# Attention with decay and a spectral mix on one core: the loads of v move from SyncE's DMA queue to GpSimd's

## The chip, the cores and the metric

The kernel runs on one core of a Trainium2 chip. The metric is the device time of one execution in microseconds. Each engine works through its own instructions in program order; a DMA is issued by an engine (here SyncE, called SP in the profile, or GpSimd, called POOL), and 16 DMA engines then move the data.

## The reference, cut to what matters

Two computations follow each other. The first is causal attention with a forgetting decay, for 8 batches and 8 heads, 576 positions, head size 64:

```python
scores = scale * np.matmul(q, k.transpose(0, 1, 3, 2))
cum = np.cumsum(np.log(np.clip(f, 0.0001, 1.0)), axis=-1)
decay = cum[:, :, :, None] - cum[:, :, None, :]
attn = softmax(where(causal, -1e9, scores + decay))
x = matmul(attn, v)          # then (batch, position, 8*64)
```

The second takes x (8 x 576 x 512), transforms it along the positions, multiplies its first 64 modes by complex matrices `w_r`, `w_i` (each 64 x 512 x 512 in float32, 64 MiB), transforms back to y, and gives `u + max(u @ w_ch, 0)` with u = x + y.

## The kernel before, in words

The order of all work is the program's order on each engine (`tc.manual_schedule()`, line 59): nothing is reordered.

**Attention, lines 442 to 493.** Two heads of one batch make a pair; there are 32 pairs, and iteration i of the main loop works on several of them at once: it loads pair i+3 (`load_qk`, `load_v`, lines 450 and 451), issues a tile of w where the plan says so (`issue_w`, line 453), scales v of pair i+1 (`scale_v`, line 455), computes the scores of pair i (`scores`, `mask`), the product with v of pair i-1 (`av`, `norm`), the transposes of q and k of pair i+1 (`trans`), the transform of pair i-2 (`dft`), and from iteration 10 on one early part of the product with w (`spec_early`, line 492).

- `load_qk` (line 99) makes two loads on GpSimd's queue, q and k of two heads, which are turned from float32 into bf16 on the way: 64 partitions, two rows of 2304 bytes read for each. Four buffers.
- `load_v` (line 110) makes four loads, two for each head: a large one of 128 x 4 rows (128 KB) and a small one of 64 rows (16 KB). A row is 64 float32 numbers, 256 bytes. They go into one of four buffers `vbuf[i % 4]`, tile name `vst` in the profile. Before the change they are issued on SyncE's queue.
- `issue_w` (line 128) makes two loads on GpSimd's queue, one of `w_r` and one of `w_i` (1 MiB read, 512 KB written as bf16 each; 128 x 4 rows). There are six buffers (`NW = 6`) for 64 such tiles. The plan (lines 439 to 441) issues one tile in each of the iterations 0 to 5, none in 6 to 10, and one in each of 11 to 32. The tile of iteration 11 takes the buffer that `spec_early` frees in iteration 10.
- `scale_v` (line 309) multiplies v by the decay weights `wT` on GpSimd, into one of three buffers `vs`, and so frees the buffer of v. It waits for v to have landed, and for `av` of three pairs before.

So GpSimd's instructions in iteration i are, in this order: q, k of pair i+3; a tile of w; scale_v of pair i+1. SyncE has only f (line 157), v, and the output at the end.

**Before the loop, lines 155 to 179.** GpSimd issues the loads of q and k of pairs 0 to 2, and between them makes the constants: the identity matrix `ident_bf`, the positions `s_i` (an iota, line 161, from which VectorE and ScalarE derive the transform's basis), `ident_f`, `trimask` and others, and then the load of `w_ch` (line 179). The calls of `load_v` for pairs 0 to 2 stand between these lines (158, 163, 167).

**Mode product, lines 497 to 607.** The remaining 42 tiles of w are loaded and multiplied with the transformed x, beside products with `w_ch`. **Output, lines 637 to 671**: the last modes are added and the result is written on SyncE's queue.

Of the kernel before, what the change touches and what calls it, by code (L numbers as in the profile page):

```python
# [23 lines left out]
def kernel(  # L24
# [11 lines left out]
    nc = tc.nc  # L36
# [73 lines left out]
    def load_v(i):  # L110
        g, b = pairs[i]
        vt = vbuf[i % VB]
        for hp in range(2):
            nc.sync.dma_start(
                vt[:, 4 * hp : 4 * hp + 4, :],
                v[b, 2 * g + hp, 0:512, :].rearrange("(c p) d -> p c d", p=128),
            )
            nc.sync.dma_start(
                vt[64 * hp : 64 * hp + 64, 8, :], v[b, 2 * g + hp, 512:576, :]
            )  # L120

# [34 lines left out]
    ft = ssb.tile([BH, S], F32, name="ft")  # L156
    nc.sync.dma_start(ft[:], f.rearrange("b h s -> (b h) s"))
    load_v(0)
    masks.make_identity(nc, ident_bf[:])
    s_i = ssb.tile([128, NSB], I32, name="s_i")  # L160
    nc.gpsimd.iota(s_i[:], pattern=[[128, NSB]], base=0, channel_multiplier=1)
    load_qk(1)
    load_v(1)
    masks.make_identity(nc, ident_f[:])
    masks.make_upper_triangular(nc, trimask[:], val=1.0, diag=True)
    load_qk(2)
    load_v(2)
    nc.gpsimd.memset(tri4[:], 0.0)
    nc.gpsimd.tensor_copy(tri4[0:64, 0, :], trimask[0:64, 0:64])
# [532 lines left out]
```

## Time and profile before

| what | value |
|---|---|
| median of 2 runs | 483.69 us (483.61 to 483.76) |
| the profiled execution: its own time | 485.75 us |
| its span, first to last instruction | 484.0 us |
| mean granted TensorE clock | 0.81 of full speed |
| busy: PE, DVE, ACT, POOL | 355.0, 263.7, 193.8, 184.1 us |
| read from HBM, written | 163.73 MB, 9.44 MB |
| v loads, large: number, KB, median time to landing | 64, 128 KB, 10.6 us |
| v loads, small | 64, 16 KB, 10.6 us |
| q and k loads | 64, 144 KB, 14.5 and 14.7 us |
| w loads | 128, 512 KB, 19.8 and 20.0 us |

How to read it: PE is TensorE, DVE VectorE, ACT ScalarE, POOL GpSimd, SP SyncE. A DMA that an engine issues appears twice: as a short instruction on the engine's timeline (its issue), and as a landing later. The DMA lines of the profile give the busy share of the 16 DMA engines in 40 slices, in tenths, and for each queue the packets, the MB written and the share of time that its packets took; the shares may add up to more than 100%, since packets of one engine overlap. The chain of waits follows the work that ended last back to what released it; a piece such as "DMA w" in it is the time from issue to landing.

### The profile page before, as it was taken

To read this page: it belongs to the slowest core of one execution; us is meant where nothing else is said; L and a number is where in the kernel's file an instruction comes from. 1 tells how busy PE (TensorE), PEld (TensorE's weight loads), DVE (VectorE), ACT (ScalarE), POOL (GpSimd) and SP (SyncE) were. 2 spreads that over 40 slices of the span, in tenths; PEclk is the share of its full clock that TensorE was granted. 3 is DMA by queue.
4 is the path that set the end of the run, shared out by engine and by line. 5 is a ranking of instruction groups with operands and counts; after the bars stand their busy time and mean duration, and the time that the engine had idled before them with its cause. 6 is when DMAs were issued, how large, how long until landed. Compare 5 with 4: busy or idle time off the path is not lost.

```text
span 484.0 us, 8618 instructions
## 1 busy us (share of the span) xinstructions
PE 355.0 (73%) x3387; PEld 175.1 (36%) x3396; DVE 263.7 (54%) x618; ACT 193.8 (40%) x300; POOL 184.1 (38%) x274
## 2 busy tenths in 40 slices
PE   1268779997686876768968577668756687986994
PEld 1135555564353533434524133223322232432331
DVE  4979988996465555747843112122120255453785
ACT  5246555674445444523502201222102255552773
POOL 8827544763544545355433322332233233200000
PEclk9999895998757667876967957787767599797998
DMA  8999999899999999999999999999999999993687
GB/s 161 203 197 198 197 198 181 137 196 197 196 196 197 197 198 197 199 197 203 206 206 207 206 206 207 206 206 206 207 206 206 206 206 208 206 206 52 238 300 245
DMA packets 121288, 96.65 MB, mean 200 GB/s; under 512 B 42336, under 2 KB 116576, under 8 KB 121248
## 3 DMA queue, kind: packets, MB, share of 16 engines
q0 software_dynamic: 77328, 77.08, 95.3%
q1 hardware_dynamic: 43920, 19.03, 19.2%
q8 instruction: 26, 0.43, 0.3%
q14 instruction: 14, 0.11, 0.1%
HBM read 163.73 MB, written 9.44 MB: 358 GB/s over the span
## 4 chain that ended last, share of the span: by engine, by line
DMA 68%; PE 14%; issue 6%; DVE 5%; POOL 3%; ACT 3%; DVEq 0%; POOLq 0%
DMA w<-in_moe_w_i_dram 41%; DMA qk<-in_k_dram 13%; DMA w<-in_moe_w_r_dram 12%; PE pav L388 2%; PE tp L299 2%; DMA out_dram<-o_sb 2%; ACT et L350 2%; PE sps L343 2%; PE U L648 1%; PE pd L415 1%; PE Z L648 1%; PE A L146 1%; POOL w L135 1%; POOL vs L312 1%; PE U L654 1%
## 5 line engine op out<-in xcount | busy, mean ns | idle before, releaser
L350 ACT ACTIVATE et<-sps 128x1024 bf16<-128x1024 f32 x96 | 94.3, 1025 | 69.2 <-PE sps L343 66.3
L135 POOL DMA_DIRECT2D w<-in_moe_w_r_dram x64 | 48.4, 756 | 118.5 <-DMA w<-in_moe_w_r_dram 41.9
L135 POOL DMA_DIRECT2D w<-in_moe_w_i_dram x64 | 47.8, 746 | 95.9 <-DMA w<-in_moe_w_i_dram 82.7
L146 PE MATMUL A<-w,XS 128*32 128x512 bf16 x512 | 50.6, 463 | 38.4 <-DMA w<-in_moe_w_i_dram 25.4
L304 DVE COPY qkT<-tp 128x640 bf16<-128x640 bf16 x64 | 49.2, 769 | 37.7 <-PE tp L299 37.6
L541 ACT CAST XW<-pxw 128x512 bf16<-128x512 f32 (+1 forms) x40 | 23.4, 585 | 106.8 <-PE pxw L534 106.8
L299 PE MATMUL tp<-ident_bf,qk 128*64 128x128 bf16 x576 | 35.6, 264 | 37.2 <-DMA qk<-in_k_dram 33.8
L388 PE MATMUL pav<-vs,et 128*128 128x65 bf16 (+1 forms) x896 | 61.2, 214 | 0.9 <-DVE et L359 0.8
L388 PEld LDWEIGHTS <-et 128*128 128x128 bf16 (+1 forms) x896 | 44.2, 115 | 29.4 <-issue 25.9
L594 DVE TENSOR_TENSOR Yb<-A,yacc 128x512 bf16<-128x512 f32 x16 | 11.1, 692 | 71.6 <-PE A L146 71.6
L534 PE MATMUL pxw<-wch,xT 128*128 128x512 bf16 (+1 forms) x152 | 45.5, 451 | 1.7 <-DVE xT L525 1.3
L343 PE MATMUL sps<-qkT 64*128 64x512 bf16 (+4 forms) x320 | 44.4, 344 | 1.7 <-DVE qkT L304 1.5
L312 POOL TENSOR_TENSOR vs<-vst,wT 128x576 bf16<-128x576 f32 x32 | 37.6, 1175 | 18.0 <-PE pav L388 12.8
L299 PEld LDWEIGHTS <-qk 128*64 128x64 bf16 x576 | 23.9, 132 | 42.9 <-issue 33.0
L578 DVE TENSOR_TENSOR XW<-pz,XW 128x512 bf16<-128x512 f32 (+1 forms) x40 | 27.0, 690 | 21.3 <-PE pz L577 21.1
L403 DVE TENSOR_TENSOR x_all<-pav,rcp 128x384 bf16<-128x384 f32 (+2 forms) x96 | 36.2, 377 | 3.4
L525 DVE COPY xT<-ptr 128x576 bf16<-128x576 bf16 x32 | 14.7, 458 | 39.7 <-PE ptr L520 39.5
L422 DVE CAST XS<-pd 128x192 bf16<-128x192 f32 x32 | 32.6, 1032 | 0.0
L146 PEld LDWEIGHTS <-XS 128*32 128x32 bf16 x512 | 10.7, 98 | 59.2 <-issue 54.0
L665 DVE SCALAR_TENSOR_TENSOR o_sb<-Z,u_sb 128x512 f32<-128x512 f32 (+1 forms) x40 | 25.6, 685 | 10.7 <-ACT u_sb L664 6.8
L415 PE MATMUL pd<-bas,x_all 128*128 128x192 bf16 (+1 forms) x160 | 28.6, 302 | 0.9 <-DVE x_all L403 0.5
L534 PEld LDWEIGHTS <-xT 128*128 128x128 bf16 (+1 forms) x160 | 17.3, 117 | 26.6 <-issue 15.2
(113 smaller groups left out, 479.6 us busy)
## 6 DMA issues: line engine op xcount, KB each, us to landing
w<-in_moe_w_r_dram POOLq DMA_DIRECT2D x64, 512.0 KB, 19.8
w<-in_moe_w_i_dram POOLq DMA_DIRECT2D x64, 512.0 KB, 20.0
vst<-in_v_dram SPq DMA_DIRECT2D x64, 128.0 KB, 10.6
out_dram<-o_sb SPq DMA_DIRECT2D x16, 512.0 KB, 2.9
qk<-in_q_dram POOLq DMA_DIRECT2D x32, 144.0 KB, 14.5
qk<-in_k_dram POOLq DMA_DIRECT2D x32, 144.0 KB, 14.7
vst<-in_v_dram SPq DMA_DIRECT2D x64, 16.0 KB, 10.6
out_dram<-o_sb SPq DMA_DIRECT2D x4, 256.0 KB, 3.2
```

Of the source, the lines that this page charges most:

```text
L135: nc.gpsimd.dma_start(w8[:, t, :, :], src[4 * u : 4 * u + 4, dc * 128 : (dc + 1) * 128, :].rearrange("m p e -> p m e"),)
L146: nc.tensor.matmul(A[32 * j : 32 * j + 32, :], lhsT=XS[:, dc, c0 : c0 + 32], rhs=w8[:, t, j, :], start=(first and t == 0), stop=(last and ...
L299: nc.tensor.transpose(tp[64 * hp : 64 * hp + 64, r - r0, :, :].rearrange("p n c -> p (n c)"), qk[:, hp, r * 64 : r * 64 + 64], ident_bf[:, :],
L304: nc.vector.tensor_copy(st[i]["T"][:].rearrange("p n (c r) -> p n c r", r=9)[:, :, :, r0:r1], tp[:, 0 : r1 - r0, :, :].rearrange("p r n c ...
L312: nc.gpsimd.tensor_tensor(vs[:, :, 0:Dh], vbuf[i % VB][:], _strided(wT[:, i, :], [[1, 9], [0, Dh]]), ALU.mult)
L343: nc.tensor.matmul(ps[:, hp, c : c + n], lhsT=KT[sl, jb * 128 : jb * 128 + 128], rhs=QT[sl, i0 : i0 + n], start=True, stop=True,)
L350: nc.scalar.activation(st[i]["et"][:, T, :, :], ps[:], ACT.Exp, scale=scale)
L388: nc.tensor.matmul(pav[:Ms, sb % 3, hp, :], lhsT=eblk(i, hp, jb, sb), rhs=rhs, start=(jb == 0), stop=(jb == sb),)
L403: nc.vector.tensor_tensor(x_all[:ns, b, lo:hi, g * 128 : g * 128 + 128].rearrange("p s (h d) -> p s h d", h=2), pav[:ns, lo % 3 : lo % 3 + ...
L415: nc.tensor.matmul(pd[:], lhsT=x_all[:ns, b, sc, g * 128 : g * 128 + 128], rhs=bas3[:ns, sc, :, :], start=(sc == 0), stop=(sc == NSB - 1),)
L422: nc.vector.tensor_copy(XS[:, g, 0 : 24 * NM].rearrange("p (m c b) -> p c m b", c=3, b=8)[:, :, :, b], pd[:])
L534: nc.tensor.matmul(pxw[:Ms, :], lhsT=xT[:, eb, sb * 128 : sb * 128 + Ms], rhs=wch[:, eb, :], start=(eb == 0), stop=(eb == NEB - 1),)
```

## The change

The four loads of `load_v` are issued by GpSimd instead of SyncE. Rows, sizes, buffers, and the place of the calls in the program stay the same.

```diff
@@ -111,11 +111,11 @@
         g, b = pairs[i]
         vt = vbuf[i % VB]
         for hp in range(2):
-            nc.sync.dma_start(
+            nc.gpsimd.dma_start(
                 vt[:, 4 * hp : 4 * hp + 4, :],
                 v[b, 2 * g + hp, 0:512, :].rearrange("(c p) d -> p c d", p=128),
             )
-            nc.sync.dma_start(
+            nc.gpsimd.dma_start(
                 vt[64 * hp : 64 * hp + 64, 8, :], v[b, 2 * g + hp, 512:576, :]
             )
```

GpSimd's instructions in iteration i are then: q, k of pair i+3; the four loads of v of pair i+3; a tile of w; scale_v of pair i+1. Before the loop, the four loads of each of the pairs 0 to 2 stand between the constants.

## The prediction

> **What bounds the kernel now.** I read the page first: is one resource full nearly all the time?
>
> ```profile
> DMA  8999999899999999999999999999999999993687
> ...
> q0 software_dynamic: 77328, 77.08, 95.3%
> q1 hardware_dynamic: 43920, 19.03, 19.2%
> ...
> DMA 68%; PE 14%; issue 6%; DVE 5%; POOL 3%; ACT 3%; DVEq 0%; POOLq 0%
> ```
>
> The DMA engines are full from 2 us to about 437 us, except near 80 to 88 us. q0 is GpSimd's queue (q, k, w), q1 is SyncE's (v, the output). POOL, which will issue the v loads, is only 38% busy; that average is taken apart below. The chain of waits, in order of time, shows how the queue is throttled:
>
> ```profile
> 118.91 16.56 DMA w<-in_moe_w_r_dram
> 135.51 0.49 issue
> 136.00 16.45 DMA w<-in_moe_w_r_dram
> 152.50 0.49 issue
> 152.98 0.77 POOL w L135
> ...
> 246.81 20.05 DMA w<-in_moe_w_i_dram
> 267.15 20.06 DMA w<-in_moe_w_i_dram
> 287.49 20.06 DMA w<-in_moe_w_i_dram
> ```
>
> A w_r load is issued 0.5 us after the w_r load of two iterations before has landed. With q, k, w_r, w_i per iteration that is the load eight places back. Later, with w alone, eight loads are in flight again: 20.34 us between pieces, 2.54 us per load. So POOL has at most eight loads out. The period in the attention stage is (152.98-118.91)/4 = 8.5 us; with w alone it is 20.34/4 = 5.1 us per tile of two loads. The timeline of POOL shows one iteration:
>
> ```profile
> 139.13 0.75 POOL L135 DMA_DIRECT2D w<-in_moe_w_i_dram  x1 [2.36 <-DMA w<-in_moe_w_i_dram]
> 139.89 1.16 POOL L312 TENSOR_TENSOR vs<-vst,wT 128x576 bf16<-128x576 f32 x1
> 141.00 0.23 POOL L315 CAST vs<-wT 128x9 bf16<-128x9 f32 x1
> 141.13 0.65 POOL L105 DMA_DIRECT2D qk<-in_q_dram  x1
> 141.78 0.61 POOL L105 DMA_DIRECT2D qk<-in_k_dram  x1
> 144.47 0.77 POOL L135 DMA_DIRECT2D w<-in_moe_w_r_dram  x1 [2.08 <-PE pav L388]
> ```
>
> POOL works 4.1 us of 8.5 and waits the rest for landings. (The releaser PE pav is only the event that came last; the chain shows the landing.) Last, the DMA view of two windows, 75.7 to 76.1 us (nearly only v moves) and 142.5 to 144.5 us (v beside w):
>
> ```profile
> q1 hardware_dynamic: 263, 0.06, 73.9%
> q0 software_dynamic: 12, 0.01, 25.9%
> ```
> ```profile
> q0 software_dynamic: 315, 0.31, 92.1%
> q1 hardware_dynamic: 315, 0.08, 29.7%
> ```
>
> Beside w the queues alternate one packet to one (315 and 315). A v packet of 256 B then takes 0.297x16x2000/315 = 30 ns; nearly alone it takes 0.739x16x400/263 = 18 ns.
>
> **The change, part by part.** Removed: 128 issues on SP (0.4 to 0.6 us each), which nothing but v waits for; worth nothing in themselves. SP keeps f and the output, whose first issue comes after 445 us. Also lost is SP's freedom: today v(i+3) goes out as soon as scale_v(i-1) has freed its buffer, an iteration ahead of POOL's order. This costs nothing by itself: on POOL v(i+3) is still issued two iterations before scale_v(i+3), 16 us against a landing time of some 8.
>
> Moved onto q0, transfers. Of the 8.5 us period w takes 5.1; q and k read 0.56 MiB against w's 2 MiB, 1.43 us at the same rate; 2.0 is left for v. A set of v (four loads) has 1152 rows, 72 per engine: 28 ns per row. In one queue the alternation is gone, and I take 18 to 20 ns, the row nearest in size: 72x19 ns = 1.37, with 0.08 for completions 1.45 us. Saving s = 0.55 us per set. Bounds: 28 ns as now, s = 0; or w's byte rate (2048 B read in 79 ns), 10 ns, s = 1.2. That a row costs more on this queue is not excluded: the nearest q0 row, of q and k, costs 88 ns, but it reads 2304 B at w's own byte rate, so I give that end little chance. From the first w load of the second batch (w6, now issued at 86.95 us) the DMA engines are full to the end of w at 437 us, and v15 to v31 lie in this stretch: 17 x 0.55 = 9.3 us less.
>
> The Trainium skill speaks against this term: DMA: Bandwidth & Descriptors, "Issuing engines are not separate DMA queues", says loads from any engine interleave on the same 16 DMA engines, and another queue saves only issue time. By it s would be 0 and only the loss worked out next would stay, some 496 us; the two windows above show the interleaving and, against the rule, a price for it of 12 ns per packet.
>
> Moved onto POOL, issues. A large v load has 512 rows, like a w load: 0.75 us; a small one has 64, and the nearest row is k's, 128 rows, 0.61. A set costs 2x0.75 + 2x0.60 = 2.7 us of POOL. An iteration grows from 4.1 to 6.8 us with a w tile and from 2.6 to 5.3 without. Where DMA sets the pace (8.5-0.55 = 8.0 us) 6.8 fits, with 1.2 to spare. The eight places now hold one iteration (q, k, four v, two w), not two: w_i goes out when the last w_i has landed, and w_r, q, k and v, some 5 us of transfer, are then still queued, so the engines do not run dry. POOL behind such a wait delays scale_v and the next q, k, but by no more than DMA itself does.
>
> It does not fit in two places. At the start the constants are made on POOL between the loads. Issues and set-up summed from the rows: q0, k0 to 2.6 us; v0 to 5.3; identity and iota to 6.0 (now 3.3), which moves the DVE chain by 2.7 us; then pairs 1 and 2, masks and wch to 18.7 (now 10.5), scale_v(0) to 20, pair 3 to 24. By then DMA was offered 4x(1.43+1.45)+2.54 = 14 us of work and stands idle for 10 us which it works through today. So w4's last load ends at 2+10 (idle)+8x1.43+8x1.45+5x5.1+2.54 = 63 us and lands at about 64.5 (1.5 us is my estimate: the q load at 81 us landed in 3.9 us with 0.65 of issue and 0.7 of transfer). Only then may w5's last load go, which is issued at 51.5 today.
>
> Second, iterations 6 to 10 load no w; PE needs some 5 to 7 us for each, and DMA only 2.9. Here POOL sets the pace. From 65.2: scale_v 1.3, five iterations of 5.3, then q, k, v of iteration 11, 4.0: w6 is issued at 97.0 instead of 86.95, when POOL was waiting for PE. That is **10 us late**. PE, fed by qk9 at about 73 us instead of 70.06, would be ready at 90. Bounds: POOL's sum alone, without waits for landings, gives 20+6x6.8+26.5+4.0 = 91.3, 4.4 us late; with s = 0, 12.4 us late (some four sets of v lie in the full part before w5); with 0.75 us for the small loads too, 15.
>
> DVE beside POOL: POOL's new 2.7 us per iteration cost DVE nothing in my sum, since DVE works 10 to 12 us in 20 where DMA is the bound. The same page ("SWDGE vs HWDGE vs iDMA") says that GpSimd's descriptor writing can be locked out by DVE; the rows here show no sign, a w issue takes 742 to 812 ns everywhere. The phase from 230 us and the tail hold no v and stay.
>
> Sum: 484.0 of span + 10.0 - 9.3 = 484.7. The profiled execution took 485.75, 2.06 above the median of the runs; carried to the median, 483.69 + 0.7 = 484.4. In general, the net is 12.4 - 21.4 s: late by 12.4 - 4.4 s, less 17 s.
>
> **The rivals.**
> Nearly even (the sum above): **484.4**, own range 478 to 491, for v rows of 16 to 24 ns.
> Slower, v rows gain nothing: if a row on POOL's queue costs what it costs today, nothing pays for the late w6: 483.7+12.4 = 496. For it: no 256 B row was ever seen on q0. Against it: 18 ns when v ran nearly alone. It decides (over 2%, 9.7 us) from s below 0.13, 26 ns per row.
> Faster, rows near w's byte rate: s = 1.2 gives 12.4-25.7 = -13, so 470.5. For it: one queue fetches in one stream; against it: the 18 ns. It decides from s above 1.03, 13 ns.
> POOL the bound throughout: if a v issue takes 1.1 us, an iteration is 8.5 us on POOL, the gain is gone and each of the iterations 6 to 11 and the start lose 1.7 more: about 508. Against it: 193 issues on q0, all between 0.59 and 0.81 us.
> That v was hidden anyway and nothing moves ends at 483.7, inside the first.
>
> **How the numbers follow.** Nearly even 0.55, no gain per row 0.28, cheap rows 0.12, POOL bound 0.05. Two per cent, about what a measurement of this kernel tells from no change, is 9.7 us: 474.0 to 493.4. Faster 0.12; slower 0.28 + 0.05, of which some 0.03 stay within: 0.30; same 0.58. The range takes in most of the second case and the edge of the third: 474 to 499.
>
> **What would show it.** Right: in the attention stage a period near 8.0 us instead of 8.5, only q0 active, POOL busy 6.8 us of it, w landing in about one period; POOL without idle from about 66 to 97 us, DMA with holes in 10 to 25 and 70 to 97 us; the first w issue after the five w-less iterations near 97 us. Wrong: a period still at 8.5 (no cheaper rows); that w issue near 90 (POOL not the bound there); v issues far from 0.6 and 0.75 us; gaps in DMA after 100 us (eight places too few).

## The result and the profile after

The changed kernel takes 500.02 us (median of 2 runs, 499.36 to 500.69) against 483.69: a ratio of 1.034, 95% interval 1.028 to 1.040. That is 16.3 us more; the forecast was 0.7 us more, with a range up to 499. The profiled execution took 499.36 us with a span of 497.6. In the table of the experiments the ratios are of fast runs alone; one execution each of e6_pad and e7_busy was in the slow state, and only the medians hold them.

From the page of the changed kernel: the DMA engines in 40 slices, the packets, the two queues (packets, MB, share), and the chain's shares.

```profile
DMA  5799996599999999999999999999999999995587
...
DMA packets 87495, 96.65 MB, mean 194 GB/s; under 512 B 5472, under 2 KB 80736, under 8 KB 87456
...
q0 software_dynamic: 82448, 86.53, 103.5%
q1 hardware_dynamic: 5008, 9.59, 5.5%
...
DMA 76%; POOL 11%; PE 7%; issue 4%; DVE 1%; DVEq 0%; POOLq 0%
```

The same bytes now go in fewer packets. q0 has 5120 packets more than before; 2048 of them are completions (128 loads on 16 engines), so 3072 carry the 36864 rows of v. That is twelve rows in a packet on average, where SP's queue made one packet of each row. New holes stand in slices 1, 2, 7 and 8 (5 to 7 tenths; each slice is 12.4 us), and POOL is now 11% of the chain, from 3%.

The chain in order of time. Each "DMA w" piece runs from issue to landing:

```profile
55.85 9.31 DMA w<-in_moe_w_i_dram
65.45 0.75 POOL w L135
...
94.07 1.10 POOL qk L105
95.17 0.49 POOL vst L114
95.96 1.30 POOL vst L114
97.25 0.53 POOL vst L118
98.02 10.05 DMA w<-in_moe_w_i_dram
108.36 8.67 DMA w<-in_moe_w_i_dram
117.31 7.57 DMA w<-in_moe_w_i_dram
125.17 7.45 DMA w<-in_moe_w_i_dram
132.91 8.87 DMA w<-in_moe_w_i_dram
142.06 8.46 DMA w<-in_moe_w_i_dram
```

Three things are seen. The last load of w5 goes out at 65.45 us (forecast 65.2; 51.5 before). From there to 98 us the chain is POOL's own instructions, one after the other: POOL sets the pace, and w6's first load goes out at 97.25 us (forecast 97.0; 86.95 before), its second at 98.02. And from 98 us on each w_i load waits for the w_i load of the iteration just before to land, where before the change it was two iterations before. POOL's timeline shows the same wait in one iteration:

```profile
134.92 0.65 POOL L105 DMA_DIRECT2D qk<-in_q_dram  x1
135.56 0.61 POOL L105 DMA_DIRECT2D qk<-in_k_dram  x1
136.16 0.80 POOL L114 DMA_DIRECT2D vst<-in_v_dram  x1
136.93 0.57 POOL L118 DMA_DIRECT2D vst<-in_v_dram  x1
137.46 0.81 POOL L114 DMA_DIRECT2D vst<-in_v_dram  x1
138.23 0.58 POOL L118 DMA_DIRECT2D vst<-in_v_dram  x1
139.63 0.78 POOL L135 DMA_DIRECT2D w<-in_moe_w_r_dram  x1 [0.82 <-PE pav L388]
142.06 0.75 POOL L135 DMA_DIRECT2D w<-in_moe_w_i_dram  x1 [1.66 <-DMA w<-in_moe_w_i_dram]
142.83 1.16 POOL L312 TENSOR_TENSOR vs<-vst,wT 128x576 bf16<-128x576 f32 x1
```

The issues of a v set take 2.7 us, as forecast. What failed to come is the gain. Take the period from the w_i issue of tile 10 to that of tile 22, twelve iterations: 132.9 to 234.7 us, 8.48 us each, against 8.50 before and 8.0 in the forecast. The v rows did become cheaper, and the packet records of this trace show it: between 135 and 195 us a packet of 16 v rows takes 210 ns on average, 13 ns a row, where before the change a packet of one row took 30 ns in the same window. Yet the period stood.

### The profile page after: what moved, and what is told of

It is laid out like the page before. It is cut to its first block, busy times and chain, and to the rows that moved or that the text cites. A ratio compares the mean times of both kernels' runs of the same rounds, so it can differ in the third digit from the quotient of the medians.

```text
span 497.6 us, 8537 instructions
## 1 busy us (share of the span) xinstructions
PE 351.7 (71%) x3396; PEld 175.7 (35%) x3396; DVE 264.8 (53%) x618; ACT 196.5 (39%) x300; POOL 266.5 (54%) x402
## 4 chain that ended last, share of the span: by engine, by line
DMA 76%; POOL 11%; PE 7%; issue 4%; DVE 1%; DVEq 0%; POOLq 0%
DMA w<-in_moe_w_i_dram 75%; POOL vst L114 3%; POOL qk L105 2%; POOL vst L118 2%; POOL vs L312 2%; PE U L648 2%; PE Z L648 2%; PE U L654 1%; POOL w L135 1%; DMA out_dram<-o_sb 1%; PE pyl L627 1%; DVE o_sb L665 0%; POOL vs L315 0%; PE pu L571 0%; PE pu L574 0%
## 5 line engine op out<-in xcount | busy, mean ns | idle before, releaser
L350 ACT ACTIVATE et<-sps 128x1024 bf16<-128x1024 f32 x96 | 96.8, 1025 | 80.6 <-PE sps L343 80.3
L135 POOL DMA_DIRECT2D w<-in_moe_w_r_dram x64 | 49.6, 774 | 83.7 <-DMA w<-in_moe_w_r_dram 17.2
L146 PE MATMUL A<-w,XS 128*32 128x512 bf16 x512 | 48.8, 446 | 40.9 <-DMA w<-in_moe_w_i_dram 26.6
L388 PEld LDWEIGHTS <-et 128*128 128x128 bf16 (+1 forms) x896 | 46.5, 115 | 78.0 <-issue 74.5
L114 POOL DMA_DIRECT2D vst<-in_v_dram x64 | 53.7, 840 | 0.2 <-issue 0.2
L402 DVE RECIPROCAL rcp<-pav 128x6 f32<-128x6 f32 (+2 forms) x96 | 16.2, 169 | 58.7 <-PE pav L388 58.1
L343 PE MATMUL sps<-qkT 64*128 64x512 bf16 (+4 forms) x320 | 45.4, 354 | 1.7 <-DVE qkT L304 1.5
L118 POOL DMA_DIRECT2D vst<-in_v_dram x64 | 39.4, 616 | 0.0
L299 PE MATMUL tp<-ident_bf,qk 128*64 128x128 bf16 x576 | 36.8, 272 | 3.1 <-DVE rcp L402 1.2
L312 POOL TENSOR_TENSOR vs<-vst,wT 128x576 bf16<-128x576 f32 x32 | 38.6, 1207 | 0.3
```

Of the source, the lines that this page charges most:

```text
L114: nc.gpsimd.dma_start(vt[:, 4 * hp : 4 * hp + 4, :], v[b, 2 * g + hp, 0:512, :].rearrange("(c p) d -> p c d", p=128),)
L118: nc.gpsimd.dma_start(vt[64 * hp : 64 * hp + 64, 8, :], v[b, 2 * g + hp, 512:576, :])
L135: nc.gpsimd.dma_start(w8[:, t, :, :], src[4 * u : 4 * u + 4, dc * 128 : (dc + 1) * 128, :].rearrange("m p e -> p m e"),)
L146: nc.tensor.matmul(A[32 * j : 32 * j + 32, :], lhsT=XS[:, dc, c0 : c0 + 32], rhs=w8[:, t, j, :], start=(first and t == 0), stop=(last and ...
L299: nc.tensor.transpose(tp[64 * hp : 64 * hp + 64, r - r0, :, :].rearrange("p n c -> p (n c)"), qk[:, hp, r * 64 : r * 64 + 64], ident_bf[:, :],
L312: nc.gpsimd.tensor_tensor(vs[:, :, 0:Dh], vbuf[i % VB][:], _strided(wT[:, i, :], [[1, 9], [0, Dh]]), ALU.mult)
```

## The experiments

I held two theories of why the period stood. **Places**: POOL's queue has at most eight loads out (in these traces its loads use eight semaphores in turn, and none is issued sooner than 0.28 us after the load eight places back has landed); with eight loads in an iteration that is one iteration, and the engines run dry between landing and next issue. **Rows**: the engines are simply full, and a v row costs on q0 what it cost beside w. The 13 ns above already speak against it. A third, **busy**, came up on the way: it is POOL's own time, not the places. In the table, "w6" is the issue of the second load of tile 6, "period" the mean over the twelve iterations named above, both from the profiled execution; the ratio is to the kernel before in the same call. One execution's w6 is no better than 2 us: e1_late runs the program of before up to w6, e2_early that of after, and they differ from these by 2.3 and 1.8 us. e5_one leaves the rows of the second head in other places than the products expect, so it shows times only and does not compute the reference's result.

| kernel | median us | ratio (95%) | loads per iteration on q0 | w6, us | period, us |
|---|---|---|---|---|---|
| before | 483.7 | | 4 | 87.7 | 8.50 |
| after | 500.0 | 1.034 (1.028 to 1.040) | 8 | 98.0 | 8.48 |
| e1_late | 486.1 | 1.005 (1.002 to 1.009) | 4, then 8 | 85.4 | 8.36 |
| e2_early | 498.1 | 1.029 (1.025 to 1.033) | 8, then 4 | 99.8 | 8.52 |
| e3_scratch | 498.0 | 1.028 (1.024 to 1.033) | 8 | 97.4 | 8.53 |
| e4_big | 475.8 | 0.983 (0.979 to 0.988) | 6 | 88.5 | 7.64 |
| e5_one | 472.8 | 0.976 (0.971 to 0.981) | 5 | 85.4 | 7.58 |
| e6_pad | 497.3 | 1.025 (1.018 to 1.031) | 8 | 98.2 | 8.28 |
| e7_busy | 484.8 | 1.002 (0.998 to 1.005) | 6 | 97.6 | 7.60 |
| e8_small | 484.0 | 1.001 (0.998 to 1.004) | 6 | 86.2 | 8.32 |
| e9_start | 491.1 | 1.015 (1.011 to 1.019) | 4, then 8 | 91.7 | 8.46 |
| e10_both | 469.6 | 0.970 (0.965 to 0.975) | 4, then 6 | 85.7 | 7.65 |

### Early or late: e1_late and e2_early

```diff
-            nc.gpsimd.dma_start(          # all pairs
+        eng = nc.sync if i < 15 else nc.gpsimd    # e1_late
+        eng = nc.gpsimd if i < 15 else nc.sync    # e2_early
+            eng.dma_start(
```

> v of pairs 0 to 14 stays on SP, v of pairs 15 to 31 goes to POOL: only the full stretch from w6 on is changed. Theory places (eight loads in flight on POOL's queue now cover one iteration, so the engines run dry between them and the cheaper rows are not cashed): the period of the stretch stays at 8.3 to 8.5 us, 483 to 487 us. Theory rows (a v row costs on POOL's queue what it costs beside w, the engines are simply full): the same. My forecast's sum would make it 9 us faster, 474 to 475.

> v of pairs 0 to 14 on POOL, the rest on SP: only the start and the iterations without w are changed. Theory places and theory rows both: w6 issued near 97 us, and the whole late part is then paid, 494 to 498 us. If the loss came from the later stretch it would be near 484.

Measured: 486.1 and 498.1 us, that is +2.3 and +14.3; together 16.6, the 16.3 of the whole change. The loss is made before w6, as the forecast's working had it, but it is 14 and not 10. The late part, which the forecast counted at -9.3, gives +2.3. The two experiments only say where; both theories foretold them alike.

### Fewer loads on the queue: e4_big and e5_one

```diff
-            nc.gpsimd.dma_start(
+            nc.sync.dma_start(            # e4_big: the small loads only
                 vt[64 * hp : 64 * hp + 64, 8, :], v[b, 2 * g + hp, 512:576, :]
             )
```
```diff
+        nc.gpsimd.dma_start(              # e5_one: instead of the four loads
+            vt[:, :, :],
+            v[b, 2 * g : 2 * g + 2, :, :].rearrange("h s d -> (h s) d").rearrange("(c p) d -> p c d", p=128),
+        )
```

> Only the two large v loads of a pair on POOL, the two small ones stay on SP: six loads of an iteration share the eight places instead of eight, 1.3 iterations, and POOL works 1.1 us less per iteration than with all four. Theory places: the period of the stretch falls to 7.5 to 8.0 us, w6 near 91 us, 474 to 484 us in all. Theory rows: the period stays at 8.4, only the earlier w6 is gained, 488 to 491.

> One load of all 1152 rows of v of a pair on POOL, so five loads of an iteration share the eight places. The rows are the same in number and size, but those of the second head come to other partitions (its 576 rows follow those of the first without a break), so the second head's v rows stand in another order than the reference's. Theory places: the engines stay full, and with rows at 10 to 13 ns the period is 7.3 to 7.6 us; w6 near 88 us; 466 to 473 us. Theory rows: period 8.4, 484 to 487 us.

Measured: 475.8 and 472.8 us, periods 7.64 and 7.58. Theory rows foretold 488 to 491 and 484 to 487 and falls. With 5.1 us for w and 1.43 for q and k, some 1.1 us is left for v, by this estimate 15 ns per row where the forecast took 19 and the rows before cost 28. POOL's timeline in e4_big shows where the eighth place now falls, on the load of k, which waits for the w_i of two iterations before:

```profile
102.15 0.66 POOL L105 DMA_DIRECT2D qk<-in_q_dram  x1
104.40 0.60 POOL L105 DMA_DIRECT2D qk<-in_k_dram  x1 [1.60 <-DMA w<-in_moe_w_i_dram]
105.36 1.54 POOL L114 DMA_DIRECT2D vst<-in_v_dram  x2 [0.35 <-issue]
106.89 0.76 POOL L135 DMA_DIRECT2D w<-in_moe_w_r_dram  x1
107.63 0.77 POOL L135 DMA_DIRECT2D w<-in_moe_w_i_dram  x1
```

And what the engines moved between 135 and 195 us, in 40 slices of 1.5 us, first after the change, then in e4_big:

```profile
GB/s 161 152 183 206 252 191 177 185 197 240 208 166 145 200 201 255 211 190 190 204 249 185 197 135 179 195 256 208 189 193 208 243 215 186 180 193 214 241 210 154
DMA packets 10906, 11.92 MB, mean 199 GB/s; under 512 B 908, under 2 KB 10453, under 8 KB 10901
...
q0 software_dynamic: 10901, 11.84, 116.8%
```
```profile
GB/s 221 200 207 204 243 220 203 202 206 239 236 200 204 210 228 251 196 205 207 229 246 205 203 213 218 239 203 204 206 219 258 204 203 214 213 256 207 205 207 222
DMA packets 12669, 12.98 MB, mean 216 GB/s; under 512 B 2023, under 2 KB 12180, under 8 KB 12662
...
q0 software_dynamic: 11382, 12.63, 117.8%
q1 hardware_dynamic: 1280, 0.26, 3.9%
```

The mean goes from 199 to 216 GB/s. After the change the slices go down to 135; in e4_big none falls below 196. The packets of both queues took 116.8% of the engines' time after the change and 121.7% in e4_big. That engines stand idle shows in the packet records: in this window fewer than 16 packets are in flight for 3.7% of the time after the change, so at least one of the 16 engines then has none. In each of the five kernels that have eight loads in an iteration here (after, e1_late, e3_scratch, e6_pad, e9_start) it is 3.3 to 6.4% of the time, in all others, before and e4_big among them, never. This is only a lower bound for the idle time, since packets of one engine overlap; besides, some packets of w take up to 1.5 us after the change (0.24 in e4_big) where the median is 0.10, and what an engine does in such a packet the records do not tell. The coarse line of tenths shows 9 throughout in both and hides it.

### Places or POOL's time: e6_pad and e7_busy

Both start from e4_big. One adds two loads without much to move, the other as much work on POOL without a load.

```diff
+        for m in range(2 if i >= 3 else 0):       # e6_pad
+            nc.gpsimd.dma_start(scr[i % VB][m][:], v[b, 2 * g, 512:576, :])
```
```diff
+        if i >= 3:                                # e7_busy
+            wv = _strided(wT[:, i, :], [[1, 9], [0, Dh]])
+            nc.gpsimd.tensor_tensor(scr[:], wv, wv, ALU.mult)
```

> The two large v loads on POOL, the small ones on SP, and from pair 3 on two more small loads per pair on POOL (64 rows of v into a scratch tile that nothing reads): again eight loads of an iteration for eight places, almost no bytes more, POOL 1.2 us more per iteration. Theory places: the period of the stretch goes from 7.5 back to 8.2 to 8.5 us, 489 to 500 us in all. Theory busy (it was POOL's own time, not the places): also slower, so the next kernel has to tell them apart. Theory rows (the small v rows on POOL's queue were the dear ones): the two scratch loads cost about 0.2 us per iteration, 478 to 482.

> The two large v loads on POOL, the small ones on SP, and from pair 3 on one more product of 128x576 numbers on POOL per pair into a scratch tile that nothing reads (1.2 us, as long as the two small issues), with no load. Theory places: the period stays at 7.5 to 7.7 us; only the iterations without w lose, 476 to 482 us. Theory busy: as slow as the kernel with two padding loads, 489 to 500.

Measured: 497.3 and 484.8 us; periods 8.28 and 7.60. POOL's timelines, e6_pad and then e7_busy:

```profile
127.20 1.10 POOL L116 DMA_DIRECT2D scr<-in_v_dram  x2
128.27 1.57 POOL L118 DMA_DIRECT2D vst<-in_v_dram  x2
129.78 0.80 POOL L139 DMA_DIRECT2D w<-in_moe_w_r_dram  x1
132.10 0.75 POOL L139 DMA_DIRECT2D w<-in_moe_w_i_dram  x1 [1.51 <-DMA w<-in_moe_w_i_dram]
```
```profile
130.25 0.61 POOL L105 DMA_DIRECT2D qk<-in_k_dram  x1 [1.64 <-DMA w<-in_moe_w_i_dram]
130.88 1.16 POOL L117 TENSOR_TENSOR scr<-wT 128x576 f32<-128x576 f32 x1
131.97 1.58 POOL L119 DMA_DIRECT2D vst<-in_v_dram  x2
133.52 0.78 POOL L140 DMA_DIRECT2D w<-in_moe_w_r_dram  x1
134.25 0.80 POOL L140 DMA_DIRECT2D w<-in_moe_w_i_dram  x1
```

The added POOL time is the same (1.10 and 1.16 us). Only the loads bring back the wait of w_i for the w_i just before, and with it the long period. So in the stretch it is the places and not POOL's time: theory busy falls there. From the landing of w6 to the landing of the last load of w e4_big takes 334.4 us, e7_busy 335.2 and e6_pad 347.0. Before w6 it is the other way round: both kernels have w6 near 98 us, 9 us later than e4_big, and e7_busy, which has only POOL's time, loses nearly as much as the one with places. I had expected e7_busy at 476 to 482; this early loss is larger than I allowed.

### The places without v, and the small loads alone: e3_scratch and e8_small

e3_scratch leaves v on SP and puts four small scratch loads on POOL; e8_small moves only the two small v loads.

```diff
+        for m in range(4):                        # e3_scratch
+            nc.gpsimd.dma_start(scr[i % VB][m][:], v[b, 2 * g, 512:576, :])
```
```diff
             nc.sync.dma_start(                    # e8_small: the large loads stay on SP
                 vt[:, 4 * hp : 4 * hp + 4, :],
...
-            nc.sync.dma_start(
+            nc.gpsimd.dma_start(
                 vt[64 * hp : 64 * hp + 64, 8, :], v[b, 2 * g + hp, 512:576, :]
```

> v stays on SP as before; four small loads per pair (64 rows into a scratch tile that nothing reads) on POOL where load_v stands. POOL gets the places and nearly the issue time of the change without its transfers. Theory places: the start and the iterations without w are late as after the change (w6 some 9 us late), and the stretch, with v still beside w, is at 8.5 to 9.0 us: 494 to 508 us. Theory rows: only the late w6 is paid, period 8.3, 490 to 494.

> Only the two small v loads of a pair on POOL, the large ones stay on SP. Six loads of an iteration share the eight places, but the rows of the large loads still alternate with w. Theory places: no gain from rows, the period stays near 8.2 to 8.4 us and the start loses some 2 us: 483 to 488 us. If the places alone made the gain of the kernel with the large loads on POOL, it would be near 476.

Measured: 498.0 us with w6 at 97.4 and a period of 8.53; and 484.0 us, 8.32. Without moving one row of v, four small loads make nearly the whole loss of the change, and nearly all of it before w6: w6 lands 11.6 us later than before, and from there to the last landing of w it is 347.5 us against 345.7. The period of 8.53 against 8.50 says one thing more: the transfers of such small loads cost little, so the 0.64 us that two of them add to e4_big's period in e6_pad are not their transfer. And six loads on the queue bring no gain as long as the large v loads stay beside w: the gain of e4_big is the cheaper rows, and the places only decide whether it is cashed.

### The start, and a faster version: e9_start and e10_both

```diff
+        eng = nc.sync if i < 4 else nc.gpsimd     # e9_start: all four loads
-            nc.gpsimd.dma_start(
+            eng.dma_start(
```

e10_both does the same to the large loads of e4_big; its small loads stay on SP.

> v of pairs 0 to 3 stays on SP (its issues stood between the constants before the loop and in iteration 0), all later pairs on POOL with four loads each. It takes the start out of the early loss. If the start matters as my forecast's working had it, w0 goes out at 14.5 us as before, w5 near 58 instead of 65.5 and w6 near 90 instead of 97.3: 491 to 494 us. If the eight places and POOL's pace in iterations 6 to 10 make the whole early loss, w6 stays near 97: 498 to 501.

> v of pairs 0 to 3 on SP; from pair 4 on the two large loads on POOL, the small ones on SP. The version with large loads on POOL without its late start. w6 already waited for PE there, so what is to be gained is 1 to 2 us: 473 to 476 us; faster than both kernels of the study either way.

Measured: 491.1 and 469.6 us. In e9_start w6 goes out at 91.7 us instead of 98.0, and its landing comes at 100.0 instead of 108.1; so some 6 to 8 of the 10 to 13 us by which w6 was late came from the four v sets that stood between the constants and in iteration 0. e10_both is faster than both kernels of the study, by 3.0% (2.5 to 3.5) than the one before. It came out 3 us below what I expected; w6 is only 2.8 us earlier than in e4_big (85.7 against 88.5), the last w load lands 2.8 us earlier (427.8 against 430.6), and the rest I did not trace.

## Why the prediction was wrong, point by point

- **What bounds the kernel, and eight loads in flight:** right. The waits after the change and in e4_big fall on the load eight places back each time.
- **POOL's issues, 2.7 us a set:** right, 2.7 us in the timeline above.
- **The late w6:** the issue was forecast at 97.0 us and came at 97.25, and e9_start confirms the part of the start. That the two agree so closely is in part luck: in e2_early, the same program up to there, the issue came at 99.0, after two waits for landings near 74 us that the forecast's sum does not have. The term is too small all the same: 10.0 us was taken, e2_early measured 14.3. At its landing w6 is 13.0 us late in both kernels (108.1 us against 95.1), so part of the loss lies between issue and landing: the second load of w6 takes 10.05 us to land (the chain above) and 8.3 in e2_early, where it took 7.3 before. Why is open. The loads of v14 now stand right ahead of it in the same queue, but they do so in e2_early too, and in e7_busy, with the large ones ahead, it takes 7.3.
- **The price of a row, 19 ns:** the direction was right, the size cautious. 15 ns is what e4_big and e5_one leave, and 13 what the packets themselves take; the gain per set, by the periods, is then 0.9 us, more than the 0.55 taken. Over the whole stretch, from the landing of w6 to the last landing of w, e4_big gains 11.3 us (334.4 against 345.7), where the forecast took 9.3.
- **The step that failed:** "w_r, q, k and v, some 5 us of transfer, are then still queued, so the engines do not run dry." They do run dry. The forecast counted -9.3 us for the stretch and e1_late measured +2.3 (in the changed kernel's own trace the stretch, counted as above, takes 347.6 us against 345.7): the cheaper rows were there, and the wait for a landing that is only one iteration old took all of it. The 5 us had to cover the lag of the landing behind the last byte, the 0.3 to 0.5 us from landing to issue, the 0.75 us of the issue, and the way to the engines; the forecast did not subtract these from the 5 us. That nothing is left for engines that are not in step is argued. e6_pad against e7_busy shows the cause as such; which engines run dry, and by how much each of these parts uses up the margin, the traces do not show, as their packets carry no engine.
- **The signs:** a period still at 8.5 was to mean "no cheaper rows", and it stood at 8.5 with rows that were cheaper. The sign that fitted, gaps in DMA after 100 us, was on the list, but the line of tenths does not show it.
- **The rivals:** the time of the second one (496) was nearest, for another reason than it gave: the rows were cheap, and the gain was lost to the places. The upper end of the range, 499, leaves room for a w6 15 us late with no gain from the rows; measured were 14.3 us (e2_early) and a loss of 2.3 (e1_late).

The page that was weighed, DMA: Bandwidth & Descriptors of the Trainium skill, section "Issuing engines are not separate DMA queues", comes out half right. Nothing was gained by the other queue as such in the change as made, as it says. But the queue does alter the price of the transfer: 28 ns a row on one side, some 15 on the other, and 475.8 us for e4_big against 483.8. The same page, section "SWDGE vs HWDGE vs iDMA", says that GpSimd's descriptors are gathered into packets of preferably up to 4096 bytes; the count here agrees exactly: 16 rows (4096 bytes) per packet for the large loads and 4 for the small give 96 packets per pair, 3072 in all, and the trace of the changed kernel has 2048 packets of 4096 bytes on q0 and 1024 of 1024 bytes more than before.

## What to carry to other kernels

POOL's queue held a fixed number of loads in all these kernels, eight, and not of bytes. Before small loads join a queue that carries large ones, count how many iterations its places will then cover, and subtract the time from a landing to the next arrival from what is still queued; if little is left, move only the large loads (e10_both, 469.6 us); merging them into one saves places too (e5_one, 472.8), if the rows can be brought into the right places, which was not tried. And where an engine both computes and issues, its average idle time says nothing about the stretches in which it sets the pace.

## What the runs showed of the hardware that I had not expected

- Many 256-byte rows in one load of GpSimd's queue go as packets of up to 16 rows; on SP's queue each row is a packet, and beside w each alternates with a w packet. In use that is some 15 against 28 ns a row; how much of it is the packing and how much the end of the alternation was not separated.
- Four loads of 16 KB per iteration that move almost nothing cost nearly as much as moving all of v (e3_scratch, 1.028 against 1.034). Their issues take some 0.57 us of POOL each, and nearly all of the loss lies before w6; what part of it the places have there was not separated.
- With the large v loads on POOL's queue, eight places that hold one iteration of loads keep the engines at 199 GB/s; six loads in an iteration let them reach 216, although the busy line shows 9 in every slice of both.
